# The last expert group's second layer read in whole rows, with throwaway products on TensorE and a new order of the whole program

## The chip, the core and the metric

The kernel runs on one core of a Trainium2 chip. The metric is device time in microseconds (us) of one execution. The core has five engines that run their own instruction lists in order and meet at semaphores: TensorE (PE, with its weight loads shown apart as PEld), VectorE (DVE), ScalarE (ACT), GpSimd (POOL) and SyncE (SP), which issues most DMAs. TensorE's clock has two levels here, 1.2 and 2.4 GHz; the profile gives the granted one as a share of the higher.

## What is computed

Three layers follow one another. The inputs are float32.

```
# 1. attention inside clusters: B=2, H=8 heads, S=768, D=64, 16 clusters
q_assign, k_assign = argmax of cosine similarity to the head's centroids
scores = q @ k.T / sqrt(D), -1e9 where q_assign != k_assign
x = softmax(scores) @ v                          # -> (1536, 512)
# 2. a gated layer, 512 -> 2048 -> 512
h = x @ w_in ; x = (h * clip(h + 3, 0, 6) / 6) @ w_out
# 3. soft mixture of 8 experts with 4 slots each
logits = x @ phi
slot_input = softmax(logits, over tokens).T @ x  # 32 slots of 512
slot_out[e] = relu(slot_input[e] @ w1[e]) @ w2[e]   # w1: 512x1024, w2: 1024x512
out = softmax(logits, over slots) @ slot_out     # (1536, 512)
```

## The kernel before

Most products are made in float16 with the operand split into a high and a low half; the experts' products are made in float32.

The work is written as some 1,100 small generators (`ev(fn, ...)`), and a long table of numbers, `ORDER`, says whose next step is emitted when. A second table, `ROOMS`, says which of a pool's buffers a tile takes. So the order of every engine's list is set by `ORDER`, and what a step waits for follows from the data and from the buffer it takes.

PSUM has two pools: `psm` (two rooms of 512 columns) and `pss` (three rooms of 2 x 512 columns).

Names in the program, in the order of time:

- `load`, `cast_hi`, `cast_lo` fetch q and k of head i and split them; head 0 is turned on TensorE (`turned`: `tq1`, `tq2`, 12 transposes each), all others by DMA (`qk1t`, `qk2t`). `as_mm` and `as_max` find the clusters (`as`, `oh`), `as_put` (ACT) writes them beside the operands. `maxq` (PE, `sm`) and `maxr` (DVE, `mxs`) find each row's maximum: six of each per head. `scores`, `exps`, `plow` and `pv` make `st`, `p`, `pp` and `acc`.
- `win`, `wout`: w_in and w_out arrive as float64 bit patterns and are narrowed on DVE and ACT (`nw`, `nt`).
- `hid`, `act`, `logits`, `colmax`, `dweights`, `dispatch`: the gated layer for 12 pairs of token blocks (`xt`, `h`, `ghl`, `gt`, `lg`, `lt`, `pe`, `z`).
- the end: `zsum`, `slot_in`, `slot_t` (`zt`, `si`, `sit`), then the experts in two groups g of four: `layer1(g, kk)` (PE, `e1_g`, four steps over the 512 inputs), `relu`, `turn` (`ht_g_i`), `layer2(0, i)` (`o2_0`), and for the last group `layer2_part(p, i)`.

Expert weights come through `fetch`, one chunk of 1 MB at a time, in the order of `chunks`, each into the room that `rooms` names for it. Two lines matter:

```
chunks += [("d", E - 4 + j, 0) for j in range(4)] + [("d", E - 4, 1)]
PARTS = [(0, 256), (256, 128), (384, 128)]
```

The last group's w2 (four experts of 1024 x 512) is thus read in column parts of 256, 128 and 128: each part is a whole product over the 1024 rows, in eight row blocks c, with a sum in PSUM of its own (`o2_1_0`, `o2_1_1`, `o2_1_2`). After each part `slots_out(p)` (`so`), and `combine(p, b)` (`po`) make these columns of the output and send them, so that the output of a part leaves while the weights of the next still arrive.

## Time and profile before

| | us |
|---|---|
| median of 3 runs | 481.71 (479.29 to 484.8) |
| the profiled execution | 475.53 |
| its span, first to last instruction | 473.7 |

The profiled execution is 1.83 us longer than its span, and 6.18 us shorter than the median of the runs. TensorE is busy for 427.5 of 473.7 us. The granted clock is 0.987 on the mean, but the profile gives it as 1.00 also for the first 31 us, where the products' own durations are those of the lower level.

### The profile page before, as it was taken

What the parts mean: (1) busy time and instruction counts of PE and PEld (TensorE: products, weight loads), DVE (VectorE), ACT (ScalarE), POOL (GpSimd) and SP (SyncE); (2) the same over time, 40 slices, a digit from 0 to 9 for tenths busy, and PEclk for the clock granted to TensorE, in tenths of its full rate; (3) what the DMA queues carried; (4) which work ended last, traced back from release to release, by engine and by line L of the source; (5) the groups of instructions that cost most, each with busy time, mean ns of one, the idle gap of its engine ahead of it and who ended that gap; (6) DMA issues with size and microseconds to landing.
All of it is one profiled execution on the core that took longest, in us unless ns stands there. A gap on an engine that the chain in (4) does not pass through costs nothing.

```text
span 473.7 us, 11606 instructions
## 1 busy us (share of the span) xinstructions
PE 427.5 (90%) x4802; PEld 271.8 (57%) x4802; DVE 283.1 (60%) x497; ACT 316.9 (67%) x518; POOL 248.8 (53%) x227
## 2 busy tenths in 40 slices
PE   2699999999979999999999998989898999889884
PEld 1357677777857466656666666654554444533353
DVE  4999999999957576375666868422244124631123
ACT  5699998899966779767889898963355336500121
POOL 4467658757534466576788897983322333030000
PEclk9999999999989999999999999999999999979999
DMA  8788959756779854584858956008998769998998
GB/s 263 212 158 213 264 102 286 167 157 229 189 242 221 182 147 86 90 136 113 179 125 127 149 119 125 1 1 135 282 412 293 167 142 342 409 396 293 345 291 274
DMA packets 133812, 95.48 MB, mean 202 GB/s; under 512 B 96384, under 2 KB 119424, under 8 KB 133760
## 3 DMA queue, kind: packets, MB, share of 16 engines
q1 hardware_dynamic: 129088, 88.95, 72.3%
q10 hardware_dynamic: 4672, 5.80, 3.5%
q8 instruction: 37, 0.61, 0.6%
q14 instruction: 15, 0.12, 0.1%
HBM read 64.06 MB, written 7.34 MB: 151 GB/s over the span
## 4 chain that ended last, share of the span: by engine, by line
PE 50%; DVE 18%; ACT 11%; DMA 8%; issue 6%; POOL 5%; DVEq 0%; ACTq 0%; SPq 0%; POOLq 0%
PE h L693 21%; DVE mxs L530 7%; PE e L1324 3%; ACT p L600 3%; PE st L552 3%; PE st L556 3%; POOL pp L341 2%; PE sm L514 2%; PE acc L622 2%; ACT pp L331 2%; POOL ghl L341 2%; DMA wk<-in_moe_w_dram 2%; DMA wod<-in_moe_w_out_dram 2%; PE z L802 1%; PE o L1361 1%
## 5 line engine op out<-in xcount | busy, mean ns | idle before, releaser
L341 POOL TENSOR_TENSOR pp<-p,pp 128x768 f16<-128x768 f32 x72 | 118.6, 1655 | 56.0 <-ACT pp L331 23.4
L693 PE MATMUL h<-wq,xt 128*128 128x512 f16 x576 | 131.6, 379 | 1.1 <-DMA xt<-xhl 1.1
L530 DVE TENSOR_REDUCE mxs<-sm 128x1 f32<-128x768 f32 x96 | 88.9, 952 | 16.5 <-PE sm L514 15.8
L693 PEld LDWEIGHTS <-xt 128*128 128x128 f16 x576 | 55.2, 98 | 62.1 <-DMA xt<-xhl 2.0
L341 POOL TENSOR_TENSOR ghl<-r,ghl 128x1024 f16<-128x1024 f32 (+1 forms) x25 | 50.3, 2012 | 61.5 <-ACT ghl L331 57.4
L600 ACT ACTIVATE p<-st 128x768 f32<-128x768 f32 x72 | 57.9, 808 | 13.2 <-PE st L556 9.8
L331 ACT ACTIVATE pp<-p 128x768 f16<-128x768 f32 x72 | 60.4, 844 | 1.2
L552 PE MATMUL st<-qk1t 128*128 128x384 f16 x192 | 48.4, 334 | 5.6 <-ACT p L600 4.0
L712 DVE SCALAR_TENSOR_TENSOR r<-r,h 128x1024 f32<-128x1024 f32 (+1 forms) x26 | 29.6, 1137 | 38.7 <-ACT r L710 38.6
L514 PE MATMUL sm<-qk2t 80*128 80x384 f16 x192 | 47.2, 339 | 4.6 <-DVE qk2t L385 1.5
L556 PE MATMUL st<-qk2t 102*128 102x384 f16 x192 | 48.7, 335 | 0.0
L710 ACT ACTIVATE r<-h,b_relu 128x1024 f32<-128x1024 f32 (+1 forms) x26 | 27.2, 1046 | 24.3 <-PE h L693 17.0
L627 PE MATMUL acc<-v,pp 128*128 128x65 f16 x432 | 36.1, 192 | 0.2 <-DVE mv L501 0.2
L622 PE MATMUL acc<-v,pp 128*128 128x65 f32 x288 | 36.2, 276 | 0.0
L628 PE MATMUL acc<-v,pp 128*128 128x64 f16 x432 | 36.1, 194 | 0.0
L622 PEld LDWEIGHTS acc<-v,pp 128*128 128x128 f32 x288 | 35.3, 195 | 1.2 <-DVE mv L501 0.3
L331 ACT ACTIVATE ghl<-r 128x1024 f16<-128x1024 f32 (+1 forms) x26 | 25.7, 988 | 14.9 <-DVE r L712 10.9
L627 PEld LDWEIGHTS <-pp 128*128 128x128 f16 x432 | 31.1, 99 | 3.3 <-DVE mv L501 0.6
L341 POOL TENSOR_TENSOR qk<-qk,qk 128x768 f16<-128x768 f32 x15 | 24.7, 1645 | 13.5 <-DMA qk<-in_q_dram 4.8
L628 PEld LDWEIGHTS <-pp 128*128 128x128 f16 x432 | 29.2, 96 | 2.7
L331 ACT ACTIVATE qk<-qk 128x768 f32<-128x768 f32 (+2 forms) x32 | 26.0, 818 | 3.7 <-DMA qk1t<-qk 2.5
L552 PEld LDWEIGHTS <-qk1t 128*128 128x128 f16 x192 | 17.3, 103 | 17.3 <-issue 11.4
(193 smaller groups left out, 756.3 us busy)
## 6 DMA issues: line engine op xcount, KB each, us to landing
wk<-in_moe_w_dram SPq DMA_DIRECT2D x60, 512.0 KB, 8.2
wi<-in_moe_w_in_dram SPq DMA_DIRECT2D x16, 512.0 KB, 6.1
wod<-in_moe_w_out_dram SPq DMA_DIRECT2D x16, 512.0 KB, 5.0
wos<-wo ACTq DMA_DIRECT2D x8, 512.0 KB, 4.3
wk<-wos SPq DMA_DIRECT2D x8, 512.0 KB, 5.5
qk<-in_q_dram SPq DMA_DIRECT2D x16, 192.0 KB, 3.3
qk<-in_k_dram SPq DMA_DIRECT2D x16, 192.0 KB, 3.4
v<-in_v_dram SPq DMA_DIRECT2D x16, 192.0 KB, 3.7
```

The lines of the kernel that those rows point to most:

```text
L331: nc.scalar.activation(out, in_, AF.Copy, scale=scale)
L341: (nc.vector if e == "v" else nc.gpsimd).tensor_tensor(out=out, in0=in_, in1=hi, op=ALU.subtract)
L514: nc.tensor.matmul(s[:, j, 0:384], d["qk2t"][0:80, n, 0], d["qk2t"][0:80, 3 * j : 3 * j + 3, 1], start=True, stop=True,)
L530: nc.vector.tensor_reduce(out=mxs[i % 2][:, 96 + n : 97 + n], in_=s[:, :, 0:384], op=ALU.max, axis=AX.XY)
L552: nc.tensor.matmul(s[:, j, 0:384], d["qk1t"][:, t, 1], d["qk1t"][:, 3 * j : 3 * j + 3, 0], start=True, stop=False)
L556: nc.tensor.matmul(s[:, j, 0:384], d["qk2t"][0 : 96 + NT, t, 1], d["qk2t"][0 : 96 + NT, 3 * j : 3 * j + 3, 0], start=False, stop=True,)
L600: nc.scalar.activation(p32, s[:, :, 0:384], AF.Exp, scale=sc_exp)
L622: nc.tensor.matmul(o, p32[:, j, r * P : (r + 1) * P], d["v32"][:, t], start=(t == 0 and n == 0), stop=False)
L627: nc.tensor.matmul(o, hi, v1[:, t, 0:65], start=(t == 0 and n == 0), stop=False)
L628: nc.tensor.matmul(o[:, 0:64], hi, v1[:, t, 65:129], start=False, stop=False)
L693: nc.tensor.matmul(s[:, fb % 2], xt[:, lhs], wq[fb][:, hl, kk], start=(n == 0), stop=(n == 11))
L712: nc.vector.scalar_tensor_tensor(out=g, in0=r, scalar=6.0 * SG, in1=sf, op0=ALU.min, op1=ALU.mult)
```

## The change

**Weights.** Row blocks 0 to 3 of the last group's w2 are four ordinary chunks of kind "2", and row blocks 4 and 5 two chunks of kind "c"; both are read two whole rows at a time, 4 KB in one piece for each partition. Row blocks 6 and 7 are still read in the three column parts, kind "d": one chunk for the first 256 columns, one for both parts of 128.

**Sums.** All three sums are open from the first row block on: `op_0` in a room of `psm`, `op_1` and `op_2` in the two halves of one room of `pss`. `layer2_rows` adds row blocks 0 to 5 to all of them, `layer2_part(p)` adds blocks 6 and 7 of part p and closes it.

**Throwaway products.** 77 new steps `keep(n, m)` take a room of `pss` and multiply two constants, 256 columns a product, 168 products in all; nobody reads them.

**Smaller edits.** `pe_11` goes to a `pss` room. `slots_out` pauses once more between its two products. `ORDER` and `ROOMS` are new throughout (2,758 numbers in place of 2,600).

```diff
+    def keep(n, m):
+        t = pss(f"kw_{n}")
+        for _ in range(m):
+            nc.tensor.matmul(t[:, 0, 0:256], ident16, ident.bitcast(F16), start=True, stop=True)
+        yield
...
-        pe = psm(f"pe_{t}")
+        pe = psm(f"pe_{t}") if t < NTOK - 1 else pss(f"pe_{t}")[:, 0]
...
-    chunks += [("d", E - 4 + j, 0) for j in range(4)] + [("d", E - 4, 1)]
+    chunks += [("2", E - 4 + j, 0) for j in range(4)]
+    chunks += [("c", E - 4, 0), ("c", E - 2, 0), ("d", 0, 0), ("d", 1, 0)]
...
+            if kind == "c":
+                t = t.rearrange("p (j c d) -> p j c d", j=2, c=2)
+                for j in range(2):
+                    src = w2[e + j].rearrange("(p c) d -> p c d", c=8)
+                    nc.sync.dma_start(t[:, j], src[:, 4:6])
...
+                for c in range(2):
+                    src = w2[E - 4 :].rearrange("e (p c) d -> c p e d", c=8)[6 + c]
+                    nc.sync.dma_start(tp[:, c], src[:, :, c0 : c0 + w])
...
+    for n in range(7):
+        ev(keep, n, 4)
...
+    for n in range(40):
+        ev(keep, 7 + n, 2)
...
+    def layer2_rows(i):
+        g = NG - 1
+        if i == 0:
+            sl["op", 0] = psm("op_0")
+            t = pss("op_1")
+            sl["op", 1], sl["op", 2] = t[:, 0], t[:, 1]
+        for c in (range(4), range(4, 6))[i]:
+            for p, (c0, w) in enumerate(PARTS):
+                for j in range(4):
+                    wr = wt_["c", E - 4 + j][:, c - 4] if i else wv("2", E - 4 + j, 0, c)
+                    nc.tensor.matmul(
+                        sl["op", p][32 * j : 32 * j + 32, 0:w], hw(g, c, j), wr[:, c0 : c0 + w], start=(c == 0), stop=False
+                    )
...
-    def layer2_part(p, i):
+    def layer2_part(p):
         c0, w = PARTS[p]
-        for c in range(4 * i, 4 * i + 4):
+        for c in range(6, 8):
...
+    for n in range(30):
+        ev(keep, 47 + n, 2)
```

What the new order does is shown at three places. First ACT near the start, from the last cast of head 0's v to the copy of `qk2t_0`; L469 and L470 (L488 and L489 in the new file) are `as_put` of head 0, `qk_1` and `qk1_1` the casts of head 1. Before:

```order
L331 ACTIVATE v1_0_107<-v32_0_110 128x6x64
L438 COPY ac_0_217<-as_0_204 128x192
L863 ACTIVATE nt_i0_0_259<-wi_0_0_256 128x1024
L331 ACTIVATE qk_1_262<-qk_1_262 128x768
L331 ACTIVATE qk1_1_273<-qk_1_262 128x6x2x64
L469 ACTIVATE qk2_0_104<-oh_0_226 128x6x16
L470 ACTIVATE qk2_0_104<-oh_0_226 128x6x16
L385 COPY qk2t_0_278<-tq2_279 128x6x128
```

And now:

```order
L457 COPY ac_0_286<-as_0_249 128x192
L344 ACTIVATE v1_0_107<-v32_0_110 128x6x64
L882 ACTIVATE nt_i0_0_288<-wi_0_0_172 128x1024
L344 ACTIVATE qk_1_302<-qk_1_302 128x768
L488 ACTIVATE qk2_0_104<-oh_0_298 128x6x16
L489 ACTIVATE qk2_0_104<-oh_0_298 128x6x16
L344 ACTIVATE qk1_1_313<-qk_1_302 128x6x2x64
L404 COPY qk2t_0_357<-tq2_358 128x6x128
```

`as_put` has moved ahead of the second cast of head 1. On PE, 96 throwaway products stand among the first 400 rows, ahead of the first `st`.

Second PE in the experts, where the last `e1` product of group 1 ends. Before, `ht_0_0` and `ht_0_1` stood 16 products earlier, in the middle of `e1_1`:

```order
L1324 MATMUL e1_1_6609<-wk_19_6589,sts_6531 32x512
L1348 MATMUL ht_1_0_6659<-ident_84,late_b0_6626 128x128 x4
L1348 MATMUL ht_1_1_6664<-ident_84,late_b0_6626 128x128 x4
L1361 MATMUL o2_0_6673<-wk_20_0_6592,late_w0_6656 32x512
L1361 MATMUL o2_0_6673<-wk_21_6596,late_w0_6656 32x512
```

And now, with `cTp` (12 transposes of the combine weights, ahead of `so_0` in the old list) and then `ht_1_1` and `ht_1_0` behind these rows:

```order
L1349 MATMUL e1_1_6776<-wk_19_6743,sts_6730 32x512
L1373 MATMUL ht_0_0_6830<-ident_84,late_b0_6819 128x128 x4
L1373 MATMUL ht_0_1_6838<-ident_84,late_b0_6819 128x128 x4
L1278 LDWEIGHTS late_a0_6826
L1278 MATMUL cTp_6844<-ident16_86,late_a0_6826 128x128
```

The turns of group 0 have moved behind the end of `e1_1`, and `cTp` between them and the turns of group 1.

Third SP's list where the last group's w2 is issued (`wk_28` to `wk_35`). Before:

```order
L1024 DMA wk_30_6706<-in_moe2_w2_dram 128x4x256
L1024 DMA wk_31_6708<-in_moe2_w2_dram 128x4x256 x2
L1024 DMA wk_27_6698<-in_moe2_w2_dram 128x1024
L1024 DMA wk_28_6701<-in_moe2_w2_dram 128x4x256
L1002 DMA wk_32_6713<-in_moe2_w2_dram 128x8x128
L1024 DMA wk_30_6706<-in_moe2_w2_dram 128x4x256
L1002 DMA wk_33_6714<-in_moe2_w2_dram 128x8x128
L1002 DMA wk_34_6715<-in_moe2_w2_dram 128x8x128
L1002 DMA wk_35_6716<-in_moe2_w2_dram 128x8x128
L1002 DMA wk_32_6713<-in_moe2_w2_dram 128x4x128
```

And now:

```order
L1045 DMA wk_31_6918<-in_moe2_w2_dram 128x1024 x2
L1045 DMA wk_27_6909<-in_moe2_w2_dram 128x1024
L1045 DMA wk_28_6911<-in_moe2_w2_dram 128x1024
L1014 DMA wk_32_6965<-in_moe2_w2_dram 128x1024
L1014 DMA wk_33_6967<-in_moe2_w2_dram 128x1024
L1045 DMA wk_29_6913<-in_moe2_w2_dram 128x1024
L1014 DMA wk_32_6965<-in_moe2_w2_dram 128x1024
L1014 DMA wk_33_6967<-in_moe2_w2_dram 128x1024
L1025 DMA wk_34_7021<-in_moe2_w2_dram 128x4x256 x2
L1025 DMA wk_35_7086<-in_moe2_w2_dram 128x4x128 x4
```

Eight MB take the same rooms in the same order; six of them now come in pieces of 4 KB, one in 1 KB and one in 512 bytes, where before four came in 1 KB and four in 512 bytes.

## Rows read from the trace of the kernel before

**Rows 1.** Busy time by stretch: PE, PEld, DVE, ACT, POOL; clock, DMA share, GB/s.
```profile
0.00:20.00 20.00, 8.73 (x77) 5.87 (x78) 12.83 (x29) 10.84 (x20) 7.60 (x46) 1.00 0.89 267
...
22.00:25.00 3.00, 0.46 (x1) 0.16 (x1) 2.93 (x7) 2.97 (x6) 2.08 (x7) 1.00 0.63 120
...
20.00:60.00 40.00, 35.24 (x359) 24.40 (x357) 38.84 (x66) 36.73 (x59) 27.29 (x22) 1.00 0.83 198
...
220.00:260.00 40.00, 40.00 (x532) 25.36 (x531) 24.51 (x48) 36.12 (x62) 32.73 (x22) 1.00 0.72 148
```

**Rows 2.** PE in order of time, the first 32 us.
```profile
13.44 1.44 PE L382 MATMUL tq<-ident,qk 128*128 128x128 f16 x12 [0.24 <-ACT qk L469]
...
25.02 0.56 PE L488 MATMUL cm<-ones,oh 128*80 128x1 f16 x6 [0.20 <-DVE oh L457]
...
29.74 0.85 PE L556 MATMUL st<-qk2t 102*128 102x384 f16 x2
30.38 0.83 PE L514 MATMUL sm<-qk2t 80*128 80x384 f16 x2
31.02 0.51 PE L552 MATMUL st<-qk1t 128*128 128x384 f16 x2
31.37 0.49 PE L556 MATMUL st<-qk2t 102*128 102x384 f16 x2
```

**Rows 3.** ACT and DVE in order of time, the first 20 us.
```profile
11.36 1.77 ACT L331 ACTIVATE qk<-qk 128x768 f32<-128x768 f32 x2 [0.87 <-DMA qk<-in_k_dram]
11.37 0.36 DVE L457 TENSOR_TENSOR oh<-as,mx 128x192 f16<-128x192 f32 x1
...
13.03 0.27 ACT L469 ACTIVATE qk<-oh 128x96 f16<-128x96 f16 x1
...
16.98 0.69 DVE L861 TENSOR_SCALAR nw_i<-wi 128x1024 uint32<-128x1024 uint32 x1
...
17.70 3.55 DVE L530 TENSOR_REDUCE mxs<-sm 128x1 f32<-128x768 f32 x4
```

**Rows 4.** DVE and PE in order of time around 135 us.
```profile
134.85 0.69 DVE L861 TENSOR_SCALAR nw_o<-wod 128x1024 uint32<-128x1024 uint32 x1 [3.55 <-DMA wod<-in_moe_w_out_dram]
...
136.75 0.72 PE L552 MATMUL st<-qk1t 128*128 128x384 f16 x2 [3.19 <-ACT p L600]
```

**Rows 5.** PE in order of time, the experts to the end.
```profile
422.93 12.20 PE L1324 MATMUL e<-wk,sts 128*32 128x512 f32 x96 [0.45 <-DVE sts L1219]
435.06 1.09 PE L1348 MATMUL ht<-ident,late_b 128*128 128x128 f32 x8
436.08 3.64 PE L1324 MATMUL e<-wk,sts 128*32 128x512 f32 x32
441.26 1.06 PE L1348 MATMUL ht<-ident,late_b 128*128 128x128 f32 x8 [1.53 <-DVE late_b L1338]
442.25 7.07 PE L1361 MATMUL o<-wk,late_w 128*32 128x512 f32 x64
449.14 4.37 PE L1381 MATMUL o<-wk,late_w 128*32 128x256 f32 x64
453.45 0.84 PE L1253 MATMUL cTp<-ident,late_a 128*128 128x128 f16 x12
...
456.83 1.93 PE L1381 MATMUL o<-wk,late_w 128*32 128x128 f32 x58 [1.30 <-DMA wk<-in_moe_w_dram]
...
463.41 1.95 PE L1381 MATMUL o<-wk,late_w 128*32 128x128 f32 x64
...
466.92 0.83 PE L1305 MATMUL po<-late_a,late_a 96*128 96x128 f16 x12 [0.68 <-DVE late_a L1289]
```

**Rows 6.** Busy time by stretch near the end, columns as in Rows 1.
```profile
424.00:426.00 2.00, 2.00 (x16) 0.65 (x12) 1.33 (x4) 0.52 (x1) 0.00 (x0) 0.50 1.01 410
...
428.00:430.00 2.00, 2.00 (x24) 0.65 (x20) 0.00 (x0) 0.00 (x0) 0.00 (x0) 1.00 0.49 123
...
450.00:452.00 2.00, 1.88 (x32) 0.90 (x28) 0.68 (x2) 0.00 (x0) 0.00 (x0) 1.00 1.18 298
```

More of the change, by code (lines that the diff above doesn't have):

```diff
@@ L986, in fetch @@
         kind, e, hf = chunks[n]
-        if kind == "d" and hf == 1:
-            ts = []
-            for j in range(4):
-                t = room(n + j, rooms[n + j], 2048, f"wk_{n + j}").rearrange("p (a c d) -> p a c d", a=2, c=8)
-                ts.append(t)
-                for a in range(2):
-                    wt_[kind, e + j, 1 + a] = (t[:, a, 0:4], t[:, a, 4:8])
-            for p, (c0, w) in enumerate(PARTS):
-                if p:
-                    np = 2 if p == 2 else 1
-                    for c in range(np):
-                        cc = slice(8 // np * c, 8 // np * (c + 1))
-                        for j in range(4):
-                            src = w2[e + j].rearrange("(p c) d -> p c d", c=8)
-                            nc.sync.dma_start(ts[j][:, p - 1, cc], src[:, cc, c0 : c0 + w])
-                            yield
+        if kind in ("c", "d"):
+            t = room(n, rooms[n], 2048, f"wk_{n}")
+            if kind == "c":
[3 more added lines that the diff above has]
+                    nc.sync.dma_start(t[:, j], src[:, 4:6])
+                    wt_[kind, e + j] = t[:, j]
+                    yield
+                return
+            for p, (c0, w) in enumerate(PARTS):
+                if (p > 0) != (e > 0):
+                    continue
+                tp = t[:, 1024 * (p == 2) :][:, 0 : 8 * w].rearrange("p (c j d) -> p c j d", j=4, c=2)
+                wt_["d", p] = tp
+                for c in range(2):
+                    src = w2[E - 4 :].rearrange("e (p c) d -> c p e d", c=8)[6 + c]
+                    nc.sync.dma_start(tp[:, c], src[:, :, c0 : c0 + w])
+                    yield
             return
@@ L1006, in fetch @@
             src = w1[e].rearrange("(p k) f -> p k f", k=4)[:, 2 * hf : 2 * hf + 2]
-        elif kind == "d":
-            src = w2[e].rearrange("(p c) d -> p c d", c=8)[:, :, 0:256]
         elif kind == "o":
@@ L1284, in slots_out @@
             )
-        yield
+            yield
         s16 = sl["s16", p] = lt2k("a1", 1 + p, [512], F16)[:, 0:w]
@@ L1373, in store2 @@
         yield
-    def layer2_part(p, i):
+    def layer2_rows(i):
[11 more added lines that the diff above has]
+                    )
+            if i == 0 and c % 2:
+                yield
+        yield
+    def layer2_part(p):
         c0, w = PARTS[p]
-        if i == 0:
-            sl["o2", NG - 1, p] = psm(f"o2_{NG - 1}_{p}")
-        for c in range(4 * i, 4 * i + 4):
+        for c in range(6, 8):
             for j in range(4):
                 nc.tensor.matmul(
-                    sl["o2", NG - 1, p][32 * j : 32 * j + 32, 0:w],
+                    sl["op", p][32 * j : 32 * j + 32, 0:w],
                     hw(NG - 1, c, j),
-                    wv("d", E - 4 + j, p, c)[:, 0:w],
-                    start=(c == 0),
+                    wt_["d", p][:, c - 6, j],
+                    start=False,
                     stop=(c == 7),
@@ L1388, in layer2_part @@
         yield
-        if i:
-            if p == 0:
-                sl["o2s", NG - 1] = lt2k("w1", NG - 1, [512], F32)
-            nc.vector.tensor_copy(sl["o2s", NG - 1][:, c0 : c0 + w], sl["o2", NG - 1, p][:, 0:w])
+        if p == 0:
+            sl["o2s", NG - 1] = lt2k("w1", NG - 1, [512], F32)
+        nc.vector.tensor_copy(sl["o2s", NG - 1][:, c0 : c0 + w], sl["op", p][:, 0:w])
+    for n in range(30):
+        ev(keep, 47 + n, 2)
     ev(zsum)
@@ L1417, in clustered_attention_ffn_softmoe @@
             ev(store2, g)
+    for i in range(2):
+        ev(layer2_rows, i)
     for p in range(len(PARTS)):
-        for i in range(2):
-            ev(layer2_part, p, i)
+        ev(layer2_part, p)
         ev(slots_out, p)
```

333 rows, old and new, of tables (ORDER, ROOMS) are left out of this document.

## The prediction

> **What bounds the kernel now.** I read the busy shares first, then the same by stretch, then the waits in order of time where a stretch shows idle time, and the chain that ended last only to see which stretches touch the end. PE is busy for 90% of the span, but it is not the one bound. From 20 to 60 us DVE is busy for 38.84 of 40 us and PE for 35.24; from 220 to 260 PE is busy for all 40 and DVE for 24.51 [rows 1]. So up to about 125 us the heads' maxima on DVE set the pace, and later TensorE. What can be gained is in three places where the bounding engine waits or runs slowly: the first 31 us, a stop near 135 us, and the experts at the end.
>
> At the start TensorE runs at 1.2 GHz, whatever the clock column says: 12 transposes of 128 columns take 1.44 us, 120 ns each, and from one pair of 384 columns to the next it is 0.64 us (29.74 to 30.38); from 31.02 on it is 0.35, and a pair lasts 0.49 in place of 0.85 [rows 2]. PE had been busy without a gap since 25.02.
>
> At the end PE waits 1.53 us for `relu` of group 1, runs at half clock for two of the experts' microseconds, and waits 1.30 us for w2 [rows 5, 6].
>
> **The change part by part.**
>
> *Start: as_put moved, and a warm TensorE.* Before, `oh` of head 0 is ready at 11.73, but ACT is in two casts of head 1 from 11.36 to 13.13, and `as_put` starts at 13.03. Then come `tq2` (1.44), two copies, `sm`, and `nw` (0.69) on DVE ahead of the first maximum at 17.70 [rows 2, 3]. After, `as_put` stands ahead of the second cast (half of 1.77, 0.88), and `nw` behind four maxima. If the products ahead lift the clock before `tq1`, `tq1` and `tq2` take half of 1.44 each. Sum, up to the first maximum: 0.88 for the cast and 0.72 for `tq2` on the path; 0.72 for `tq1`, of which the `nw` that DVE now does ahead of `as` takes back 0.69; 0.3 for a pair of `sm` (0.85 less 0.49); 0.69 for the `nw` that moves behind, which is not saved, only put off; the second cast now stands ahead of the copy of `tq2`, but beside `tq2` itself. That is 0.88 + 0.72 + 0.03 + 0.3 = 1.9 us, and about 0.5 more because the k of head 1, which ACT waited for 0.87 us, is issued two places earlier on SP. I take 2.4 us. The bounds are 3.6 (the sum with no second `nw` and the whole 0.87) and 0 (DVE finds other waits before 60 us; it has only 1.2 us of idle time there, so what is won ahead should last). Once won, it is kept: the DVE and PE lists behind it have the same steps in nearly the same places, and PE takes over as the bound.
>
> *The throwaway products at the start* (96 of 168 stand ahead of the first `st`). At 2.4 GHz one of 256 columns costs about 0.12 us by the pairs (0.35 us for 768 columns), at 1.2 about 0.21 (0.64) [rows 2]. PE is idle for 11.3 of the first 20 us and for 2.5 of the three from 22 to 25 [rows 1], and its own work there shrinks as the clock rises. 18 of them at 0.21 fill the time from the first constant to `tq1`, the other 78 take 9.4 us at 0.12. That fits, so I take 0; the other case is a rival.
>
> *Those in the middle* (ten steps, 20 products from head 14 to block 9): 2.4 us if none meets idle time. They stand where PE waited for POOL and for transposes, so I take 0.3, bounds 0 and 2.4.
>
> *Those behind the last product* (14 steps, 28 products): 3.4 us at the higher clock, 6 at the lower. The last `po` ends at 467.75 [rows 5], and the span, with the last stores, 6 us later. They lie beside that: 0, or at most 1 us at the lower clock.
>
> *The experts on PE.* From the first `e1` on: 64 products at 3.64 us for 16 [rows 5] are 14.56. Before, three quarters of them took 12.20 in place of 10.92; the clock was at 0.50 in that stretch [rows 6]. The four throwaway steps between `si` and `e1` fill the gap ahead of it, and I count on them. Then two turns (1.09), `cTp` (0.84), two turns (1.06): 17.6 in all, with `relu` (two reads of PSUM, the 1.53 of the wait) hidden behind 1.9 us of turns and `cTp`. Before, it was 19.3 (422.93 to 442.25). This gives 1.7 us.
>
> *The second layer and the outputs on PE.* Before, from 442.25 to 467.75: 25.5 us. After: `o2_0` 6.9; row blocks 0 to 5, three quarters of 4.37 + 1.93 + 1.95 [rows 5], 6.2; the rest of part 0, 1.1; its copy, `so_0` and the two casts behind it, 1.6; its `po`, 1.4; the rests of parts 1 and 2, 1.0; `so_1` and `so_2` with copies and casts, 2.0; 24 `po` at 0.83 for 12, 1.7; two throwaway steps, 0.4; and 0.7 because eight results are now copied out of PSUM in one go. Sum 23.0, so 2.5 us less: mostly the wait of 1.30 and the two closing parts, which shrink from 1.93 and 1.95 to a quarter.
>
> *The DMA that this needs.* Before, the 512-byte pieces come at 298 GB/s, with queues full (share 1.18), the whole pieces at 410 (share 1.01) [rows 6]. Of eight chunks, three leave the 512-byte kind (1.05 MB each: 3.5 us at 298, 2.6 at 410) and three the 1 KB kind, so 3 to 5 us are saved. The hole at 428 (123 GB/s), when SP waited for rooms that `e1` still read, shrinks with the faster `e1`. The last weights then land near 456, when PE reaches row block 6; the wait of 1.30 goes and nothing new is late.
> The Trainium skill speaks against this gain: its page "DMA: Bandwidth & Descriptors", section Specifications, puts the smallest transfer at line rate at 512 bytes, so that the old parts were already at full speed. Here 298 stands against 410, so the trace disagrees; by the rule the tail would come out as in the first rival.
>
> *The outputs by DMA.* Parts 1 and 2 now leave together, four stores of 384 KB in place of two at the end: up to 2.6 us more by 298 GB/s for two more stores, less what was already in flight before. I take 0.8.
>
> *pe_11 and the pause in slots_out:* 0, since the room of `pss` is free there and the two `so` stand together.
>
> **Sum:** -2.4 + 0.3 - 1.7 - 2.5 + 0.8 = -5.5 us. The profiled execution of 475.53 would become 470.0. The median of the runs lies 6.2 us above that execution; I carry this over: 481.71 - 5.5 = 476.2.
>
> **The rivals.**
>
> *Whole rows arrive no faster*, the queue being full either way. Against it: 410 beside 298. For it: the share above 1 in both stretches. Then the last weights land only some 1.5 us earlier (the smaller hole), and the end follows them: 2.4 - 0.3 + 1.2 = 3.3 us, 478.4.
>
> *Slower: the clock does not rise at the start.* TensorE's clock took until 31 us to rise, though PE was busy for 8.73 of the first 20. If the throwaway products run at 0.21, the 96 take 20.2 us. Of the idle time, 11.3 + 2.5 us, some 1.7 lie ahead of the first constant; 12.1 are left, so `st`, and with it ACT, POOL and DVE, come 8.1 us later in place of 2.4 earlier. With the tail's 3.4 the time is 481.7 + 8.1 + 0.3 - 3.4 = 486.7. It decides from 0.13 us for a product on the mean (12.1 over 96). Against it: the gapless stretch from 25.02 was enough.
>
> *Another wait in the new order.* DVE stopped 3.55 us for w_out at 134.85, and PE 3.19 us behind it [rows 4]: SP could issue that load only when DVE had emptied its room, and the consumer stands nine DVE steps later. In the new list it again stands nine steps later, so I leave the stop in. A second one of that size elsewhere gives 476.2 + 3.2 = 479.4; the stop gone gives 473.0, since ACT's read stands four steps later now.
>
> *The change does not do what it says:* excluded for the fetch by SP's list; for the clock it is the second rival.
>
> **How the numbers follow.** The forecast 0.50, with its own range 471.5 to 479; rows no faster 0.16; the clock low 0.08; a new wait 0.12; the stop gone 0.14. The range 469.5 to 481.5 leaves out the low clock, and some of the edges of the others. A measurement of this kernel can tell about 1%, 4.8 us. Below 476.9 lie 0.6 of the forecast (its middle and its better half), nearly all of the stop gone, and a fifth of the rest but the low clock: 0.30 + 0.13 + 0.06, and a little more as the runs of before spread upward, where a clock that falls would put them: 0.54. Above 486.5 lies half of the low clock and small tails: 0.08.
>
> **What would show it.** Right: the first maximum on DVE near 15.3 us; `tq2` at about 0.75 us; no stretch at 0.5 after 418 us; no wait for `relu`; whole-row weights near 400 GB/s; last weights before 457; the last `po` near 461.5. Wrong: throwaway products of 0.2 us ahead of `st`, or `sm` and `st` waiting for the `pss` rooms that they take; a wait for w2 in `op`; a long tail of stores; or a stop of DVE on a load in the first 140 us that is longer than the one of before.

## The result, and the profile after

| | before | after |
|---|---|---|
| median of 20 runs each | 479.98 us (476.04 to 489.66) | 482.66 us (477.89 to 486.21) |
| ratio, 95% interval | | 1.0072, 1.0046 to 1.0097 |
| the profiled execution, its span | 475.53, 473.7 | 478.89, 477.1 |

The change makes the kernel slower by 0.7%. The ratios, here and below, leave out runs more than 1.5% above the fastest of their kernel, and the medians do not. Forecast were 476.2 us and a range of 469.5 to 481.5; the median lies above it.

Milestones of the two profiled executions show where the 3.4 us of the span arise. Nothing is lost behind `zsum`, though 3.4 us were to be won there.

| us | before | after | after - before |
|---|---|---|---|
| first maximum of head 0 (DVE `mxs`) | 17.70 | 16.53 | -1.17 |
| first `st` on PE | 26.58 | 28.89 | +2.31 |
| first maximum of head 4 | 65.03 | 66.21 | +1.18 |
| first `h` (gated layer) | 155.70 | 157.27 | +1.57 |
| `zt`, behind `zsum` | 413.05 | 416.44 | +3.39 |
| first `o2_0` | 442.25 | 442.39 | +0.14 |
| first output store issued | 460.40 | 463.28 | +2.88 |
| last expert weights landed | 463.59 | 461.79 | -1.80 |
| span | 473.65 | 477.10 | +3.45 |

**The start.** Busy time by stretch, after, columns as in [rows 1]:

```profile
0.00:20.00 20.00, 15.72 (x144) 11.80 (x144) 13.21 (x29) 12.00 (x23) 8.27 (x47) 1.00 0.85 248
20.00:23.00 3.00, 1.54 (x21) 0.95 (x20) 2.86 (x5) 2.50 (x4) 0.76 (x2) 1.00 0.93 264
22.00:25.00 3.00, 2.56 (x14) 1.26 (x13) 2.73 (x8) 1.68 (x3) 2.28 (x3) 0.67 0.16 55
26.00:28.00 2.00, 1.89 (x17) 1.20 (x16) 1.94 (x3) 1.75 (x3) 0.00 (x0) 0.50 1.28 164
```

PE in order of time, after, answering to [rows 2]:

```profile
13.57 0.83 PE L401 MATMUL tq<-ident,qk 128*128 128x128 f16 x12
...
21.49 0.47 PE L447 MATMUL as<-ct,qk1t 128*128 128x32 f16 x12 [1.19 <-DMA qk1t<-qk]
...
22.80 2.76 PE L363 MATMUL kw<-ident,ident 128*128 128x256 f16 x10
...
28.55 0.50 PE L447 MATMUL as<-ct,qk1t 128*128 128x32 f16 x12
28.89 0.80 PE L571 MATMUL st<-qk1t 128*128 128x384 f16 x2
...
30.00 0.49 PE L571 MATMUL st<-qk1t 128*128 128x384 f16 x2
```

The throwaway products do warm the clock: `tq2` takes 0.83 us in place of 1.44 (1.47 in e3 below, the same order without them). But the granted clock then falls to 0.50, the lower level, from 23.0 on for 6.8 us. From 20 to 23 us PE had been busy for 1.54 us, with a wait of 1.19 for the transpose of head 1; most of the 2.56 us of the next row lies behind the fall, where ten products take 2.76 us. And the first `st` is late all the same. Why shows in ACT, DVE, POOL and the sequencer of SP (SPq, the issue of DMAs), after, answering to [rows 3]:

```profile
12.84 0.28 ACT L488 ACTIVATE qk<-oh 128x96 f16<-128x96 f16 x1 [0.30 <-DVE oh L476]
...
13.20 0.83 ACT L344 ACTIVATE qk<-qk 128x768 f16<-128x768 f32 x1
...
19.97 1.28 ACT L308 ACT_TABLE_LOAD   x1
...
21.55 0.84 ACT L344 ACTIVATE qk<-qk 128x768 f16<-128x768 f32 x1
```

```profile
16.53 1.82 DVE L549 TENSOR_REDUCE mxs<-sm 128x1 f32<-128x768 f32 x2
```

```profile
14.11 1.65 POOL L354 TENSOR_TENSOR qk<-qk,qk 128x768 f16<-128x768 f32 x1 [0.86 <-ACT qk L344]
...
22.46 1.64 POOL L354 TENSOR_TENSOR qk<-qk,qk 128x768 f16<-128x768 f32 x1 [2.24 <-ACT qk L344]
```

```profile
15.78 1.93 SPq L423 DMA_TRANSPOSE qk1t<-qk  x1
...
24.13 1.43 SPq L423 DMA_TRANSPOSE qk1t<-qk  x1
```

Head 1's second cast (ACT, 13.20) now stands behind `as_put`. POOL makes the low half from it (14.11), then the transpose is issued (15.78, before 14.88), and PE's `as` of head 1 waits for it until 21.49. Head 2 goes the same way from 21.55, behind a load of ACT's function table, and its `as` (28.55) stands just ahead of the first `st`.

**The middle.** DVE and PE, after, answering to [rows 4]:

```profile
93.07 1.40 DVE L880 TENSOR_SCALAR nw_o<-wod 128x1024 uint32<-128x1024 uint32 x1 [1.56 <-DMA wod<-in_moe_w_out_dram]
...
137.29 0.69 DVE L880 TENSOR_SCALAR nw_o<-wod 128x1024 uint32<-128x1024 uint32 x1 [1.35 <-DMA wod<-in_moe_w_out_dram]
```

```profile
95.52 0.81 PE L533 MATMUL sm<-qk2t 80*128 80x384 f16 x4 [2.04 <-DVE qk2t L558]
...
139.18 0.49 PE L571 MATMUL st<-qk1t 128*128 128x384 f16 x2 [1.46 <-ACT p L619]
```

The stop of 3.55 us on w_out is now shorter (1.35), and a new one stands at 93: DVE waits 1.56 us for the first chunk of w_out, and PE 2.04 behind it.

**The end.** Busy time by stretch, after, answering to [rows 6]:

```profile
424.00:426.00 2.00, 1.74 (x14) 1.17 (x18) 1.25 (x4) 0.00 (x0) 1.82 (x12) 1.00 1.03 404
428.00:430.00 2.00, 2.00 (x24) 0.65 (x20) 0.00 (x0) 0.00 (x0) 0.00 (x0) 1.00 1.03 412
450.00:452.00 2.00, 1.62 (x14) 0.35 (x6) 0.69 (x1) 0.00 (x0) 0.00 (x0) 1.00 1.03 409
462.00:464.00 2.00, 2.00 (x30) 1.34 (x27) 1.27 (x3) 1.08 (x2) 0.00 (x0) 1.00 0.00 0
```

PE in order of time, after, answering to [rows 5]:

```profile
425.56 13.94 PE L1349 MATMUL e<-wk,sts 128*32 128x512 f32 x128 [0.17 <-DVE sts L1244]
439.43 1.09 PE L1373 MATMUL ht<-ident,late_b 128*128 128x128 f32 x8
440.76 0.83 PE L1278 MATMUL cTp<-ident,late_a 128*128 128x128 f16 x12 [0.24 <-ACT late_w L1376]
...
442.39 3.64 PE L1386 MATMUL o<-wk,late_w 128*32 128x512 f32 x32
...
453.26 2.36 PE L1410 MATMUL op<-wk,late_w 128*32 128x256 f32 x52 [1.65 <-DMA wk<-in_moe_w_dram]
...
458.90 0.64 PE L1421 MATMUL op<-wk,late_w 128*32 128x256 f32 x8 [0.72 <-DMA wk<-in_moe_w_dram]
459.47 1.35 PE L1303 MATMUL so<-late_w,late_a 128*96 128x256 f32 x4
461.75 1.03 PE L1330 MATMUL po<-late_a,late_a 96*128 96x256 f16 x8 [0.92 <-DVE late_a L1314]
...
466.48 1.62 PE L1330 MATMUL po<-late_a,late_a 96*128 96x128 f16 x21 [0.47 <-DVE late_a L1314]
...
469.01 3.22 PE L363 MATMUL kw<-ident,ident 128*128 128x256 f16 x28
```

The stage from `e1` to `o2_0` does what was forecast: 16.83 us, the clock at 1.00, no wait for `relu`; and the weights come at 404 to 412 GB/s without the hole at 428. Yet PE waits 1.65 us for w2 at 453.26 and 0.72 at 458.90, and from the first `o2_0` to the end of the last `po` it takes 26.8 us, where before it took 25.5 (442.25 to 467.75). No output is ready before all sums are nearly closed, and from 462 to 464 the DMA queues carry nothing. Before, two of three parts had left PE by then.

### The profile page after: what moved, and what is told of

Same layout as the page of the kernel before. It is cut to its first block, busy times and chain, and to the rows that moved or that the text cites. A ratio compares the mean times of both kernels' runs of the same rounds, so it can differ in the third digit from the quotient of the medians.

```text
span 477.1 us, 11933 instructions
## 1 busy us (share of the span) xinstructions
PE 442.0 (93%) x4970; PEld 285.4 (60%) x4970; DVE 285.1 (60%) x497; ACT 318.2 (67%) x518; POOL 249.8 (52%) x227
## 4 chain that ended last, share of the span: by engine, by line
PE 56%; DMA 15%; ACT 11%; DVE 8%; POOL 4%; issue 3%; SPq 1%; ACTq 0%; POOLq 0%; DVEq 0%
PE h L712 23%; DMA wk<-in_moe_w_dram 6%; PE st L571 4%; PE st L575 4%; DVE mxs L549 4%; PE sm L533 3%; POOL pp L354 3%; PE acc L641 3%; DMA qk<-in_k_dram 2%; ACT pp L344 2%; ACT p L619 2%; DMA wod<-in_moe_w_out_dram 2%; PE acc L654 2%; PE acc L647 2%; PE acc L646 2%
## 5 line engine op out<-in xcount | busy, mean ns | idle before, releaser
L712 PE MATMUL h<-wq,xt 128*128 128x512 f16 x576 | 133.3, 382 | 0.6 <-DMA xt<-xhl 0.6
L549 DVE TENSOR_REDUCE mxs<-sm 128x1 f32<-128x768 f32 x96 | 88.1, 950 | 14.2 <-PE sm L533 13.4
L533 PE MATMUL sm<-qk2t 80*128 80x384 f16 x192 | 44.5, 325 | 7.9 <-DVE qk2t L558 2.5
L571 PE MATMUL st<-qk1t 128*128 128x384 f16 x192 | 47.1, 327 | 2.5 <-ACT p L619 1.5
L575 PE MATMUL st<-qk2t 102*128 102x384 f16 x192 | 47.1, 326 | 0.0
L363 PE MATMUL kw<-ident,ident 128*128 128x256 f16 x168 | 28.3, 300 | 2.8 <-POOL ident L313 1.8
L533 PEld LDWEIGHTS <-qk2t 80*128 80x128 f16 x192 | 17.6, 99 | 19.7 <-issue 9.2
```

The lines of the kernel that those rows point to most:

```text
L533: nc.tensor.matmul(s[:, j, 0:384], d["qk2t"][0:80, n, 0], d["qk2t"][0:80, 3 * j : 3 * j + 3, 1], start=True, stop=True,)
L549: nc.vector.tensor_reduce(out=mxs[i % 2][:, 96 + n : 97 + n], in_=s[:, :, 0:384], op=ALU.max, axis=AX.XY)
L571: nc.tensor.matmul(s[:, j, 0:384], d["qk1t"][:, t, 1], d["qk1t"][:, 3 * j : 3 * j + 3, 0], start=True, stop=False)
L575: nc.tensor.matmul(s[:, j, 0:384], d["qk2t"][0 : 96 + NT, t, 1], d["qk2t"][0 : 96 + NT, 3 * j : 3 * j + 3, 0], start=False, stop=True,)
L712: nc.tensor.matmul(s[:, fb % 2], xt[:, lhs], wq[fb][:, hl, kk], start=(n == 0), stop=(n == 11))
```

## The experiments

**Theory A**, after reading the two traces: the throwaway products behind the start, at the lower clock, stand on PE's path. **Rivals**: the casts and transposes of heads 1 and 2 are late; the stop at 93 costs; the tail costs. Ratios are to the kernel before, with 95% intervals.

### Which half: the order of the layers or the end

**e1: the old order up to the first step of `zsum`, the new end behind it**, with its 40 throwaway products.

```diff
-ORDER = <before, to the end>
+ORDER = <before, up to zsum> + <after, from zsum on>
```

> The order of before up to the first step of zsum (no throwaway products there, pe_11 in its old room), the changed kernel from there on: whole rows, three sums, its throwaway products around the experts and behind the last po. Theory A (the loss is made in the first 30 us, where throwaway products run at half clock and put the first st 2.3 us later, and the new tail by itself is worth little, since its first store starts only when nearly all weights have landed): the last weights land near 458, the first store at 460, the end 1 to 3 us before that of the kernel before, ratio 0.994 to 0.998. Theory B (the new tail is the loss: all sums close together and the outputs leave late): ratio 1.005 to 1.010, first store still 2 us later than before. My prediction's tail (-3.4 us) would give 0.993.

Measured: 0.9991 (0.9955 to 1.0027), 478.63 us.

**e2: the reverse**, the new order and its throwaway products up to `zsum`, the old column parts behind it.

> The changed order and its throwaway products up to the first step of zsum, from there on the kernel before (column parts, its order, no throwaway products). Theory A: zsum 2.4 to 3.5 us later than in before, and the weights of the last group as much later behind it: ratio 1.005 to 1.008. Theory B: the delay is absorbed by the wait for weights, ratio 0.998 to 1.002. My prediction's start (-2.4 us) would give 0.995.

Measured: 1.0066 (1.0022 to 1.011), 482.67 us, as slow as the whole change. So the loss comes with the new order of the layers ahead of `zsum`, and the new end, worth 3.4 us in the sum, is worth nothing that a measurement tells. In e2 that order also brings its own `ROOMS` (353 of 828 tiles have another room than before), `pe_11` in its new room and 128 throwaway products. Runs below take the products out; none changes the rooms alone, so what is called the order here is the order with its rooms.

### The throwaway products

**e3: none of the 168.** **e4: only the 20 between 21.8 and 28.5 us taken out.** **e16: e1 without those in its end.**

```diff
 def keep(n, m):
+    if n in (22, 23, 35, 29, 11, 18, 39, 13, 42, 38):   # e4; e3 and e16: always
+        return
     t = pss(f"kw_{n}")
```

> The changed kernel without any of the 168 throwaway products; order, rooms and all else as in it. Theory A: the first st comes 2 us earlier (near 26.8 in place of 28.89), tq1 and tq2 take 1.44 again, the first e1 products run at half clock but beside a full DMA queue: 1.5 to 2.5 us less than the changed kernel, ratio to before 1.002 to 1.004. Rival (the throwaway products do their work and the order is what costs): slower than the changed kernel by 1 to 3 us, ratio 1.009 to 1.013.

> The changed kernel without the 20 throwaway products that stand between as of head 1 (21.5 us) and the first st; the others stay. Theory A: these ran at 0.5 of the clock for 4.7 us ahead of the first st, so it comes 2 to 2.3 us earlier, and that stays to the end: ratio to before 1.002 to 1.003. Rival (they lift the clock at 30 us, and without them the scores run at half clock for longer): the st pairs of the first 8 us take 0.85 in place of 0.49, less than 0.7 us is left of the gain, ratio 1.006 to 1.008.

> The first run's kernel without the throwaway products of its tail (some 40, ahead of e1, among the po and behind the last). If the experts only run up against the weights (PE waited 2.70 us for w2 there): e1 runs partly at half clock again, 1 to 1.5 us longer, the wait for w2 shrinks by as much, the first store comes within 0.7 us of 462.1, ratio within 0.002 of that run's 0.999. My prediction (1.7 us gained in the e1 stage by the warm clock): 1.002 to 1.003.

Measured: e3 1.0048 (1.0003 to 1.0093), e4 1.0175 (1.0124 to 1.0227), e16 0.9991 (0.9952 to 1.003). PE of e4 in order of time:

```profile
28.33 0.50 PE L449 MATMUL as<-ct,qk1t 128*128 128x32 f16 x12 [1.60 <-DMA qk1t<-qk]
28.67 0.80 PE L573 MATMUL st<-qk1t 128*128 128x384 f16 x2
...
29.90 0.85 PE L573 MATMUL st<-qk1t 128*128 128x384 f16 x2
```

Without the products PE is idle for 1.60 us ahead of the same `as`, and `st` starts 0.22 us earlier. Theory A falls: the products lie in time in which PE waits for the transpose. The kernel without any is still slow (483.00 us), so they are not the loss; and e16 equals e1, so in the end they give nothing that these runs can tell. e4 came out slower than both expectations, 486.32 us in six runs. The sign that its rival named is there: without the 20 products the clock stays at the lower level from 22.4 to 32.6 us, with them to 29.8, and a pair of `st` at 30 us lasts 0.85 in place of 0.49. By these figures that is at most 1.4 us, half of the 2.8; why e4 loses more is open.

### The start

**e5: the second cast of head 1 ahead of `as_put`** (ACT's list):

```diff
+L344 ACTIVATE qk1_1_313<-qk_1_302 128x6x2x64
 L488 ACTIVATE qk2_0_104<-oh_0_298 128x6x16
 L489 ACTIVATE qk2_0_104<-oh_0_298 128x6x16
-L344 ACTIVATE qk1_1_313<-qk_1_302 128x6x2x64
```

**e6: e5, and on SP the load of v of head 1 behind q, k of head 2 and `wi_1_0`**, since SP waited for v's one buffer ahead of them. **e9: e6, and ACT's table load behind the casts of head 2.** **e10: the kernel before with `as_put` moved alone.**

> The changed kernel, but the second cast of head 1 stands ahead of as_put of head 0 on ACT again, as before. Theory C (the first st waits for as of head 2, and that for a chain that begins with this cast: POOL's low half of head 1, the DMA transpose qk1t_1, which frees the one buffer for the casts of head 2, their low half, qk1t_2): qk1t_1 is issued near 14.9 in place of 15.78, qk1t_2 lands 0.9 to 2 us earlier than 28.50, the first st comes at 26.9 to 28.0, and the ratio to before is 1.003 to 1.006. Rival (throwaway products at half clock hold it back): first st unchanged within 0.3 us of 28.89, ratio 1.007.

> As the run before, and on SP the load of v_1 (which waits for the one buffer of v until 10.2 us) stands behind q and k of head 2 and wi_1_0, with v_1's first cast behind head 2's on ACT. Theory C: the weights no longer fly beside qk1t_1, which lands 4.5 us after its issue in place of 5.7, so the first st comes at 26.3 to 27.0, ratio 1.001 to 1.004. Rival: first st near 28.9, ratio 1.007.

> The changed kernel with the cast of head 1 ahead of as_put, the loads of head 2 ahead of v_1's, and ACT's table load (1.28 us) behind the casts of head 2 instead of ahead of the second. Theory C (two gates stood before head 2's cast at 21.5 us: the landing of qk1t_1 and this table load): the cast starts near 20.0, qk1t_2 is issued near 22.7, the first st comes at 26.6 to 27.4 in place of 28.89; ratio 1.001 to 1.004. Rival (something else on the new order's way to the first st): it stays above 28.2, ratio 1.005 to 1.008.

> The kernel before with one edit of the change alone: as_put of head 0 ahead of the second cast of head 1 on ACT. My prediction: up to 0.9 us gained (first maximum on DVE at 16.8 in place of 17.70, and it stays). Theory C: that cast is the head of the chain to head 2, so qk1t_1 is issued 0.5 to 0.9 us later and the first st comes 0.3 to 0.9 us later than 26.58, ratio 1.000 to 1.003; with half of it hidden, 0.999 to 1.001.

Measured: e5 1.005 (1.0015 to 1.0085), e6 1.0072 (1.0039 to 1.0104), e9 1.0103 (1.0066 to 1.0139), e10 0.9993 (0.9957 to 1.0029). The first `st` came at 28.56, 29.36, 27.36 and 26.22. By its median (481.48 us, where the kernel before had 478.80 beside it) e9 is no slower than the change. ACT of e9:

```profile
27.99 1.28 ACT L308 ACT_TABLE_LOAD   x1
...
30.34 1.50 ACT L612 ACTIVATE pp<-st 128x768 f32<-128x768 f32 x2
```

In e6 the transpose of head 1 landed 2 us earlier (19.39 in place of 21.44), and the table load, now at 20.66, held head 2's cast until 22.07. In e9 the casts were free and the load, at 27.99, held the first `pp`. Each mending moved the wait to the next step, and none of them moved the time in the way it moved `st`. So the time of the first `st` hardly shows in the whole: e9 has it 1.5 us earlier than the change and is as slow, and e10 had the first maximum 0.37 us and the first `st` 0.36 us earlier and is equal to before. In e5, e6 and e9 the first maximum of head 4 still comes at 66.3 to 67.6 us, before at 65.03.

**e13: the old order for 40 us, then the new. e14: the new for 40 us, then the old, new end.**

> The order of before up to the first maximum of head 2 (about 40 us, no throwaway products until there), then the changed order to the end. If the loss of the changed order is made in the first 40 us (first st 2.3 us later): the stop at 93 us comes 2 us earlier and costs as much, ratio 0.998 to 1.002. If it is made later (the stop on w_out at 93 us and what follows): ratio 1.005 to 1.008. If half and half, 1.002 to 1.005.

> The other way about: the changed order with its 96 throwaway products up to the first maximum of head 2, then the order of before to zsum, then the changed tail. If the loss is made in the first 40 us: ratio 1.004 to 1.008. If later: 0.997 to 1.001.

Measured: e13 1.0262 (1.0203 to 1.0321), e14 1.0009 (0.9954 to 1.0063). The seams made stops of their own (DVE 3.4 us and PE 2.47 at 47 to 51 us in e13, 2.73 at 50 in e14), so e13 tells nothing by its size. e14 pays for its seam and is not measurably slower than before, but the interval reaches to 1.0063, and by the medians it is 482.59 to 479.88 us. So it speaks against the new first 40 us as the whole loss and does not settle it. The profiles show part of the delay early: without these two, the first maximum of head 4 comes at 64.5 to 66.8 us in the eight with the old order (median 65.4), and at 65.2 to 69.8 in the ten with the new one (median 67.5).

### The stop at 93 us

**e7: DVE reads the first chunk of w_out seven DVE steps later. e8: e6 and e7 together.**

```diff
-L880 TENSOR_SCALAR nw_o_0_1605<-wod_0_1600 128x1024
 L558 SCALAR_TENSOR_TENSOR qk2t_1496<-sm_5_1579,nident 6x6x128
...
+L880 TENSOR_SCALAR nw_o_0_1683<-wod_0_1600 128x1024
```

> The changed kernel, but DVE's first read of the first w_out chunk stands seven DVE steps later (behind three maxima of head 6). Theory D (the new order has a new stop at 93 us, 1.56 us of DVE and 2.04 of PE, behind which the clock falls in some runs): the stop is gone or under 0.5 us, ratio 1.002 to 1.005. Rival (it is given back anyhow, as heads further on wait for w_out at 137 us): the delay at 145 us is the same 0.6 us, ratio 1.006 to 1.008.

> All three edits of the runs before in the changed kernel. If the starts and the stop are the whole of what the new order loses against the old one, the first step of zsum comes at the time of before (413 us) or up to 2 us ahead of it, and the ratio is that of the old head with the new tail, 0.996 to 1.001. If there is more in the order than these places, 1.002 to 1.006.

Measured: e7 1.0025 (0.9986 to 1.0064), e8 1.0037 (1.0 to 1.0074). Better than 1.0072, but the intervals overlap. In e7 the stop did not go away: PE waited 2.38 us at 97.30 for the transposes of the next head.

In many profiles of the new order the granted clock falls behind this stop. Busy time by stretch of e2:

```profile
98.00:102.00 4.00, 4.00 (x28) 3.00 (x28) 2.19 (x4) 1.85 (x3) 0.00 (x0) 0.50 0.00 0
```

It fell between 94 and 102 us, for 3.4 to 10.2 us, in nine of the eleven profiles with the new order, and in none of the nine with the old. PE's stop there was 1.5 to 3.6 us long. A stop of 2.03 or 2.04 us was followed by a fall in e5 and e13 and by none in the change and e6. The old order has a fall of its own behind its stop at 135, in six of the eight profiles apart from e18 (its expectation below says seven); from the first maximum of head 4 to the first `h` the median of the lower clock is 3.4 us with the old order and 6.8 with the new.

**e17: the last throwaway step moved from the end into this stop**, ahead of the `sm` that waits, with 18 products in place of 2, in a room of `psm`.

```diff
-        t = pss(f"kw_{n}")
-        for _ in range(m):
+        t = pss(f"kw_{n}") if n != 76 else psm(f"kw_{n}").rearrange("p (a b) -> p a b", a=1)
+        for _ in range(m if n != 76 else 18):
```

> The changed kernel with 18 throwaway products (2.0 us at the higher clock) between the last st ahead of the stop at 93.5 us and the first sm behind it, in a free room of psm; PE waited 2.04 us there. Eight of ten profiles of the new order show the granted clock at 0.50 for 6.8 or 10.2 us from 94 to 102 us, none of the old order. If this fall is what the stop costs (some 3.4 us on the median from the first maximum of head 4 to the first h): no fall there, 90.5 to 91.5 us from that maximum to the first h, ratio 1.000 to 1.004. If the fall has another cause, or the stop itself is the cost: 93 us or more in the profile, ratio 1.006 to 1.009.

Measured: 1.0083 (1.0048 to 1.0119). PE of e17 in order of time, and its busy time by stretch:

```profile
94.64 2.13 PE L363 MATMUL kw<-ident,ident 128*128 128x256 f16 x18
98.44 0.81 PE L533 MATMUL sm<-qk2t 80*128 80x384 f16 x4 [1.67 <-DVE qk2t L558]
```

```profile
102.00:104.00 2.00, 2.00 (x13) 0.99 (x11) 2.00 (x4) 0.91 (x2) 0.00 (x0) 0.55 0.03 8
```

The products ran at 0.12 us and ended before the wait did; PE stood for another 1.67 us, and the clock fell at 100.4 all the same, for 3.4 us. As a remedy it failed. It does not show what the fall costs.

**e18: the kernel before with DVE's (and ACT's) first read of the third chunk of w_out behind two more DVE steps of head 7**, to shorten its stop at 135.

```diff
-L861 TENSOR_SCALAR nw_o_0_2160<-wod_0_2147 128x1024
 L498 TENSOR_SCALAR mv_116<-cm_2124,emp_2143 16x65
 L501 SCALAR_TENSOR_TENSOR mv_116<-cm_2124,emp_2143,mv_116 16x64
+L861 TENSOR_SCALAR nw_o_0_2247<-wod_0_2147 128x1024
```

> The kernel before with one edit: DVE's and ACT's first reads of the third w_out block's first chunk (the stop at 134.85 us, 3.55 us of DVE, 3.19 of PE, with the clock at 0.50 for 3.4 to 10.2 us behind it in seven of eight profiles) stand behind the scores of head 7 that they held up. If the stop and the fall go: 2 to 4 us faster, ratio 0.992 to 0.996. If the next reader of w_out or of a room takes the wait over, as in the repair of the stop at 93 us: 0.998 to 1.002.

Measured: 1.0044 (1.0009 to 1.008), against both expectations. DVE's wait shrank from 3.55 to 2.66 us, but the clock fell for 6.8 us at 146.5, where before it fell for 3.4 at 136.9, and the first `h` came 3.5 us later. The median clock of its runs is 0.973 against 0.980.

### The end

**e11: e1 with the whole rows read as two halves of 1 KB a piece. e15: e1 with row blocks 4 and 5 in column parts too (four of eight). e12: e1 without the last 2 MB of w2**; row blocks 6 and 7 of its second layer use the weights of blocks 4 and 5.

```diff
 # e11
-nc.sync.dma_start(t[:, j], src[:, 4:6])
+for x in range(2):
+    nc.sync.dma_start(t[:, j, :, 256 * x : 256 * x + 256], src[:, 4:6, 256 * x : 256 * x + 256])
 # e15
-chunks += [("c", E - 4, 0), ("c", E - 2, 0), ("d", 0, 0), ("d", 1, 0)]
+chunks += [("d", 0, 0), ("d", 0, 1), ("d", 1, 0), ("d", 2, 0)]
 # e12
-nc.sync.dma_start(tp[:, c], src[:, :, c0 : c0 + w])
...
-wt_["d", p][:, c - 6, j],
+wt_["c", E - 4 + j][:, c - 6, c0 : c0 + w],
```

> The first run's kernel (old head, new tail), with the last group's six whole-row chunks each fetched in two halves of 256 columns, in pieces of 1 KB in place of 4 KB: same bytes, rooms and readers, twice as many DMAs. If the size of a piece sets the rate (1 KB at 329 to 361 GB/s in the kernel before, whole rows at 410): the last weights land 2 to 4 us later than 460.3, and so does the end: ratio 1.003 to 1.007. The first rival of my prediction (whole rows no faster): no change, 0.999.

> The first run's kernel (old head, new tail) with row blocks 4 to 7 of the last group's w2 in column parts in place of 6 and 7 (2 MB for the first 256 columns in 1 KB pieces, 1 MB for each part of 128), blocks 0 to 3 still in whole rows. If the end follows the closing of the first sum (3.1 MB of outputs need 12.5 us behind the first store): the first part's weights land about 2.5 us earlier, the first store near 459.8 in place of 462.1, the last weights up to 1 us later than 460.3, the end 1 to 2 us earlier, ratio 0.995 to 0.998. If the last weights set it: no gain or 1 us lost, 0.999 to 1.002.

> The first run's kernel without the fetch of the last 2 MB (row blocks 6 and 7 of the last group's w2; row blocks 4 and 5 are multiplied in their place). If the arrival of weights sets the tail: last weights at 456, the closing products 3 to 4 us earlier, the first store near 459 in place of 462.1, and the end 3 to 4 us earlier: ratio 0.990 to 0.993. If the outputs' own chain or the stores set it: under 1.5 us, ratio 0.996 to 0.999.

Measured: e11 1.0051 (1.0008 to 1.0094), e15 1.0007 (0.9964 to 1.005), e12 0.9977 (0.993 to 1.0023). The same stretch in e1, then in e11:

```profile
442.00:450.00 8.00, 7.33 (x102) 2.91 (x90) 0.69 (x1) 0.00 (x0) 0.00 (x0) 1.00 1.03 416
```

```profile
442.00:450.00 8.00, 7.58 (x102) 3.04 (x94) 0.69 (x1) 0.00 (x0) 0.00 (x0) 1.00 1.09 358
```

The rate goes with the size of a piece: 416 GB/s at 4 KB, 358 at 1 KB, with the queues as busy. e11 also issues twice as many DMAs for these chunks; in the kernel before, 438 to 442 us carry 1 KB pieces alone in DMAs of the whole size, and the rate is 346 to 358 GB/s there too:

```profile
438.00:440.00 2.00, 1.73 (x18) 0.26 (x8) 0.00 (x0) 0.21 (x1) 0.00 (x0) 1.00 1.11 358
440.00:442.00 2.00, 0.74 (x7) 0.77 (x8) 1.29 (x2) 0.94 (x3) 0.00 (x0) 1.00 1.10 346
```

So whole rows stream faster where the queues are full. What that is worth in time is less sure: the intervals of e11 and e1 overlap (medians 480.77 and 478.63 us), and e11's last weights landed at 461.38, e1's at 460.30, with `zsum` 2.6 us later in e11. PE of e1, then of e15, then of e12:

```profile
452.03 5.20 PE L1408 MATMUL op<-wk,late_w 128*32 128x256 f32 x87 [2.70 <-DMA wk<-in_moe_w_dram]
```

```profile
459.02 1.03 PE L1320 MATMUL po<-late_a,late_a 96*128 96x256 f16 x8 [0.92 <-DVE late_a L1304]
...
468.87 1.61 PE L1320 MATMUL po<-late_a,late_a 96*128 96x128 f16 x21 [0.47 <-DVE late_a L1304]
```

```profile
454.25 1.32 PE L1303 MATMUL so<-late_w,late_a 128*96 128x256 f32 x4
```

In e1 PE reaches row blocks 2 and 3 before their weights and stands for 2.70 us. In e15 the first part's `po` start 6 us earlier, counted from `zsum`, than in e1, and its first store leaves ahead of the last weights (460.55 and 463.51). The landing of the last store, counted so, comes only 0.8 us earlier: it follows the last weights by 14.6 us (e1 14.3, after 14.2; before 9.1, where only the last part's 12 `po` remained). In e12 the last weights land at 451.49 and the span is 471.7, 4.0 us under that of e1; its median is 0.8 us under, and the intervals overlap, so the times do not settle how much the weights hold up.

## Why the prediction was wrong

Two steps failed. The first is "Once won, it is kept: the DVE and PE lists behind it have the same steps in nearly the same places". By `zsum` the new order is 3.4 us late where 2.1 were to be won, and with this half alone the kernel is as slow as with all of it (e2). The second is the tail, -3.4 us in the sum: with this half alone the kernel equals before (e1). Its term that was missed by most is the -2.5 for the second layer on PE. The two profiled executions, cut at the ends of the prediction's terms:

| stretch | forecast, us | after - before, us |
|---|---|---|
| start to `zt` (start, products in the layers) | -2.1 | +3.4 |
| `zt` to first `e1` | 0 | -0.8 |
| first `e1` to first `o2_0` | -1.7 | -2.5 |
| first `o2_0` to end of last `po` | -2.5 | +1.3 |
| last `po` to end of span | +0.8 | +2.0 |

**1. Start, -2.4 us** (its upper bound of 3.6 adds up to 3.5). The part up to the first maximum was right in kind and half in size: 1.17 us, with `tq2` at 0.83 (0.72 forecast by halving, "about 0.75" named as the sign). For the first `st` the step that failed is "the second cast now stands ahead of the copy of `tq2`, but beside `tq2` itself". It looked at who waits for ACT in head 0, and not at what hangs on the cast that was put back: POOL's low half, a transpose by DMA (4.5 us before, 5.7 after), `as` of head 1, and through ACT head 2. The first `st` lost 2.31 us (table). The measured loss does not follow it, though: no mending of it brought the time back (e5, e6, e9), and e10 shows nothing of what it won. "Once won, it is kept" failed further on: the lists behind are not the same, and by head 4 the order is late also where the first `st` was mended (e9).

**2. Throwaway products.** At the start the products do not hold up the first `st`, in another way than argued: PE waits for a transpose there (e4). They are not worth 0 either, as e4 is slower without 20 of them, by more than its trace explains. The 0.3 in the middle is not contradicted by one pair of executions: from the first `h` to `zt` it is 259.17 us with the twenty products and 259.00 in e3 without, with 2.9 us more of idle time (3.4 and 2.1 us of lower clock in them). 0 for those at the end is right: the 28 end at 472.2, ahead of the last store's landing at 476.0. The rival of a cold clock was wrong in its size, though the clock fell at 23.0.

**3. "Another wait in the new order", given 0.12, is the nearest to what happened**; the forecast had the stop at 135 stay alone. The stop has shrunk to 1.35 us at 137, and there is a new one at 93. Its price was put at 3.2 us, one wait of PE. What it and the rest of the new order cost was read from the profiles, without those of e3, e7 and e16 (their executions are among the runs that the ratios leave out), in two stretches. The last two columns take off, for each stretch of lower clock, half its length, which is the most that PE can lose there (a bound, since DVE sets part of the pace).

| median of the profiles, us | first maximum of head 4 to first `h` | first `h` to `zt` | the first, low clock taken off | the second, so |
|---|---|---|---|---|
| old order (8 profiles) | 90.8 | 257.4 | 89.1 | 257.1 |
| new order (9 profiles) | 94.2 | 258.8 | 91.1 | 258.4 |

So with the bound taken off the new order is still 2.0 + 1.3 = 3.3 us longer, and with its clock as it came 4.8; ahead of these stretches it is some 2 us late already (65.4 and 67.5). These are single executions, and they add up to more than the timed loss. Beside this stands what the timed runs say. Within each kernel a run is 3.4 us longer for each 0.01 that its mean granted clock is lower (one slope for all kernels and all runs, 3.0 over the runs that the ratios take in; -0.91 is the correlation over the runs of before). Brought to a clock of 0.980 by that slope, the means are 479.4 us for before, 478.5 to 480.1 for e1, e10 and e16, and 483.2 for the change, 483.3 for e3, 482.1 to 482.7 for e5 to e9. For e2, the new order with the old end, it is 481.0, and 481.9 for e14. The runs of the change have no lower clock than those of before (medians 0.9825 and 0.980). So the falls of the clock behind the stop are not the whole loss: some 2 us (e2) to 4 us (the change) are there at equal clock, and by e1 and e2 they come with the order ahead of `zsum`. For e18 it is the other way: at 0.980 it is 478.6, below before, and its loss goes with the clock. This is a comparison and not a cause: a stop costs time and is followed by a lower clock, and no run here holds the one and changes the other.

Which places of the list, or which rooms, make this loss is open. The stop at 93 is one candidate, and taking it later (e7) gave some of it back, within the uncertainty; e17 gave nothing. In the first stretch DVE has the pace and PE's idle time between the first maximum of head 4 and the last of head 7 doubles (4.17 us after, 2.17 before), in several small waits beside the one of 2.04.

**4. Experts on PE, -1.7 us:** right, even under the forecast, 16.83 us for 17.6. In the whole it shows nowhere (e16, without the throwaway products, equals e1). Behind it PE reaches w2 earlier and waits, 1.65 + 0.72 us after, 2.70 in e1, where 1.30 was to go; that the weights set the pace there is what these waits suggest, and e12's times do not settle it.

**5. Weights near 456.** They landed at 461.79. The rate was right in the stretches shown (404 to 412 GB/s; 410 was assumed) and with it the rival of whole rows no faster is refuted. The Trainium skill, page "DMA: Bandwidth & Descriptors", section Specifications, puts the smallest transfer at line rate at 512 bytes; here 298 GB/s at 512 bytes [rows 6], 358 at 1 KB and 416 at 4 KB speak against it. What the step left out is when the fetch starts: at 420 us 76.71 MB had been moved, before 78.75. These 2 MB are 5 us at 410 GB/s, a lag of the new order up to there, whose bytes I had not added up. Nor did the stream keep its rate: from 420 us to the last weights it moved 14.1 MB at 323 GB/s before, 15.6 at 373 after, and 13.5 at 335 in e1. In e1, with the old order in front, the last weights still landed at 460.30; the whole saving of pieces and hole is 3.3 us there, near the 3 to 5 named, where "near 456" asked for 7.6.

**6. The second layer and the outputs, -2.5 and +0.8 us,** measured +1.3 and +2.0. The forecast had the weights there (near 456) before PE closes the parts; they landed at 461.79. Three sums that stay open until the last two row blocks push nearly every output behind the last weights: 14.2 us from there to the landing of the last store against 9.1, so 5.1 us more. That is more than the 3.3 us that e1's weights came earlier; e1 equals before. That the late closing is the cause is argued from the traces. e15, which closes the first sum ahead of the last weights, gained nothing: the other two parts still close together behind them.

## What to carry to other kernels

A wait that is removed ahead of a stream of weights can be counted as won only if the weights land earlier too; add up the bytes that have arrived at the start of the stage before pricing any of its work. An output that is split into parts lets early parts leave during the fetch: a change that closes all parts at once moves their tail behind the last load, whatever it wins in the rate, and letting only the first part go early did not bring it back here (e15). And where an order of a thousand steps is replaced as a whole, one stop that shrinks says little; exchange the halves of the order first, as e1 and e2 did, with their rooms if these are new too, and look at the granted clock of the runs beside their times.
